# Reordering the operations of pairs 0 to 17 in a fused attention and feed-forward kernel

## The chip, the cores and the metric

The kernel runs on one core of a Trainium2 chip. The metric is device time in microseconds (us) of one execution; lower is better. Three executions of the kernel before were timed, and one was profiled.

## What is computed

The reference is a cosine attention over 8 batches, 12 heads, 448 positions and 64 elements a head, followed by a feed-forward block with a hard-swish:

```python
q_n = q / (np.linalg.norm(q, axis=-1, keepdims=True) + 1e-06)
k_n = k / (np.linalg.norm(k, axis=-1, keepdims=True) + 1e-06)
scores = np.matmul(q_n, k_n.transpose(0, 1, 3, 2)) / tau
attn = softmax(scores)                              # over the last axis
x = matmul(attn, v)  ->  (8 * 448, 12 * 64)          # heads side by side
h = x @ w_in                                        # 768 -> 2048
g = h * np.clip(h + 3.0, 0.0, 6.0) / 6.0
out = g @ w_out                                     # 2048 -> 768
```

Inputs and output are float32; the kernel multiplies in bfloat16.

## The kernel before

Heads are worked on two at a time: a batch has 6 pairs, the kernel 48 (pairs 0 to 47). Queries and keys come as items: item j holds the queries or the keys of two pairs, so items 2d and 2d+1 serve pairs 2d and 2d+1. The inverse norms of an item are taken along its elements, the item is scaled by them, transposed by TensorE (later ones by a transposing DMA), and copied out of PSUM as query and key tiles. A pair then has four groups of scores, four exponentials, four groups of values accumulated in one PSUM tile (PV), a division by the softmax sum, and a transpose back into xT, the input of the feed-forward block. When all six pairs of a batch are in xT, the first product of that batch can run (16 units, one per 128 columns of w_in, six matmuls each); each unit is evicted by ScalarE (relu, line 589) and then VectorE (product, line 595). When these are done, the second product follows.

Every operation of pairs 0 to 17 is written out by hand in a list of text lines, PLAN (lines 21 to 60). The function run takes its words in order, and do calls the function that the word names. Each engine has a queue in program order, so the order of the words is the order in every queue: TensorE, VectorE (v), ScalarE (a), GpSimd (p), and SyncE, which issues the loads of q, k, v and the transposing DMAs. Weight loads are issued by GpSimd. No scheduler moves anything; engines wait for each other by semaphores. From pair 18 on a loop issues the work (line 1012), and it is the same in both kernels.

The words that matter here, with numbers of items (j), pairs (i) or double items (d):

- LQ.j loads an item (line 197), LV.d the values of two pairs (line 212), W one piece of the weights (line 923).
- SQ.j.engine.first.n squares n columns of item j (lines 227 and 229); RE.j sums the squares on VectorE (line 241); NO.d takes the inverse norms of two items, with four steps on ScalarE (lines 269 to 276), or with a v at the end two steps on ScalarE and two on VectorE (lines 272 and 273). NO.0.0 and NO.0.1 are those of items 0 and 1 alone. NM.j.engine scales the item (line 286), with one more number for a half of it.
- TR.j transposes an item on TensorE (line 332) and XD.j by DMA; CQ.i and CK.i copy query and key tiles of a pair (lines 352 and 354), CS.i the rest of the keys. VC.i casts the values of a pair (line 305).
- SC.i.g are the four score groups of a pair (lines 432 and 435), EX.i.g their exponentials on ScalarE (line 453), VA.i.g the value groups (line 475), FI.i the division on VectorE (lines 495 and 496), BK.i and CX.i the transpose back and its copy into xT (line 509), XP and XB the same by DMA.
- U is the next feed-forward unit on TensorE (line 580 for the first product, line 627 for the second), UA and UV its next evictions on ScalarE and VectorE. The first 30 units are of the first product, the last six of the second.
- DP.n is n dummy matmuls on zeros (line 935), D.n the same with more columns (line 930). WS sums pieces of w_out and GL copies columns on VectorE for the later second product (lines 702 and 571).

Until the last exponential of pair 5 the scores use two double buffers of PSUM; from OPEN on they share a ring of six banks with the units, the transposes of items and the transposes back:

```python
m = [psum_m.tile([128, 512], FP32, name=f"M{n}", tag=f"M{n}") for n in range(4)]
ring.extend([m[0], m[1], Y, Z, m[2], m[3]])
```

A bank is taken again only when its readers of before are done. PV is one tile, so VA of a pair waits for FI of the pair before. The list of words that moves has only the function run and the table OPS between it and the engines.

Of the kernel before, what the change touches and what calls it, by code (L numbers as in the profile page):

```python
# [1110 lines left out]
```

## Time and profile before

| | |
|---|---|
| timed executions | 404.6, 406.22 and 406.69 us, median 406.22 |
| profiled execution, first to last instruction | 404.4 us (no time of its own beside this span is given) |
| TensorE busy | 393.7 us, 97% |
| VectorE busy | 288.7 us, 71% |
| ScalarE busy | 276.7 us, 68% |
| GpSimd busy | 236.7 us, 59% |
| bytes moved by DMA | 63.75 MB, mean 158 GB/s |

The timed executions include what lies around the span. Times inside the profile count from the first instruction. A row of a timeline gives the start, the time from the start of the first to the end of the last instruction of the row, the engine, the line, the operation, output and input, the number of instructions, and in brackets how long the engine sat idle before it and what ended that. Matmuls are pipelined and their ends are modelled, so the starts of successive rows, not their lengths, give the rate.

### The profile page before, as it was taken

The numbers are of one execution on the slowest core, as the hardware profiler recorded it, in microseconds if no ns is written. First come the engines' busy times: TensorE is split into PE (matmuls) and PEld (weight loads), VectorE is DVE, ScalarE is ACT, GpSimd is POOL, SyncE is SP. The second block draws the span as 40 slices with busy tenths as digits, with TensorE's granted clock in tenths as the row PEclk, the third lists the DMA queues.
The fourth block names the chain that finished last, engine by engine and source line by source line (L and its number), as shares of the span: only waits on it lengthen the run. The fifth ranks groups of instructions, "written<-read, shape, count | busy, mean of one in ns | idle before, by whom it ended". The sixth has DMA issues, their size and how long they took to land.

```text
span 404.4 us, 9618 instructions
## 1 busy us (share of the span) xinstructions
PE 393.7 (97%) x3689; PEld 234.5 (58%) x3689; DVE 288.7 (71%) x512; ACT 276.7 (68%) x604; POOL 236.7 (59%) x232
## 2 busy tenths in 40 slices
PE   7798999999999999999999999999999999999996
PEld 5566656555665555655555556555565556555564
DVE  5898787878498777777857887587656666655663
ACT  4899989887377687687768768768758755225230
POOL 4799945862744997588486875876664600510070
PEclk9999999999999999999999999999999999999999
DMA  8899999999877748786779659986863523140134
GB/s 285 247 235 243 221 221 213 170 219 202 181 168 179 167 111 209 185 222 129 169 200 194 140 149 163 180 190 136 193 147 76 112 45 63 36 88 20 25 74 99
DMA packets 93166, 63.75 MB, mean 158 GB/s; under 512 B 56128, under 2 KB 93120, under 8 KB 93120
## 3 DMA queue, kind: packets, MB, share of 16 engines
q1 hardware_dynamic: 87408, 56.45, 61.1%
q0 software_dynamic: 5312, 6.29, 9.5%
q8 instruction: 29, 0.48, 0.6%
q10 hardware_dynamic: 400, 0.39, 0.3%
q14 instruction: 17, 0.14, 0.1%
HBM read 45.61 MB, written 11.01 MB: 140 GB/s over the span
## 4 chain that ended last, share of the span: by engine, by line
PE 88%; ACT 4%; DVE 3%; DMA 3%; SPq 1%; issue 0%; DVEq 0%; ACTq 0%
PE M L580 23%; PE M L753 16%; PE PV L475 11%; PE Y L580 6%; PE Z L580 6%; PE M L435 6%; PE Z L753 5%; PE Y L753 4%; PE M L833 3%; PE M L627 3%; ACT at L453 3%; DMA big<-in_q_dram 3%; PE Y L435 1%; PE Z L435 1%; PE Y L833 1%; PE Y L627 1%
## 5 line engine op out<-in xcount | busy, mean ns | idle before, releaser
L453 ACT ACTIVATE at<-M 128x448 bf16<-128x448 f32 x194 | 96.8, 564 | 23.2 <-PE M L435 20.7
L580 PEld LDWEIGHTS <-w_in_sb 128*128 128x128 bf16 x768 | 72.3, 98 | 63.1 <-issue 2.5
L580 PE MATMUL M<-xT,w_in_sb 128*128 128x448 bf16 x504 | 107.4, 352 | 0.1
L286 POOL TENSOR_TENSOR nrm<-big,r 128x896 bf16<-128x896 f32 (+1 forms) x47 | 78.1, 1665 | 14.8 <-issue 4.6
L229 POOL TENSOR_TENSOR big<-big 128x896 f32<-128x896 f32 (+5 forms) x45 | 68.1, 1519 | 14.8 <-DMA big<-in_k_dram 8.2
L589 ACT ACTIVATE u<-M,bias 128x448 bf16<-128x448 f32 x84 | 54.9, 655 | 26.3 <-PE M L580 26.0
L475 PEld LDWEIGHTS <-at 128*128 128x128 bf16 (+1 forms) x1536 | 54.1, 97 | 19.9 <-issue 12.1
L595 DVE SCALAR_TENSOR_TENSOR gT<-u,M 128x448 bf16<-128x448 bf16 x73 | 44.6, 617 | 29.2 <-ACT u L589 28.4
L475 PE MATMUL PV<-vx,at 128*128 128x65 bf16 (+1 forms) x1536 | 62.7, 194 | 0.0
L241 DVE TENSOR_REDUCE n<-big 128x14 f32<-128x896 f32 (+1 forms) x50 | 51.5, 1037 | 0.3 <-ACT big L227 0.2
L392 POOL COPY km<-tT 64x128 bf16<-64x128 bf16 x34 | 14.4, 424 | 61.9 <-PE M L435 25.9
L782 POOL TENSOR_TENSOR big<-big 128x384 f32<-128x384 f32 x11 | 11.8, 1077 | 54.6 <-ACT big L801 54.5
L753 PEld LDWEIGHTS <-gT 128*128 128x128 bf16 x288 | 27.8, 98 | 20.0 <-DVE gT L731 0.6
L753 PE MATMUL M<-w_out_sb,gT 128*128 128x384 bf16 x192 | 35.0, 326 | 0.1
L496 DVE TENSOR_TENSOR on<-PV,rc 128x512 bf16<-128x512 f32 x48 | 33.2, 691 | 1.7
L435 PE MATMUL M<-tT,kz 64*128 64x448 bf16 (+1 forms) x171 | 30.9, 351 | 0.5 <-ACT at L453 0.5
L453 ACT ACTIVATE at<-Y 128x448 bf16<-128x448 f32 x50 | 28.2, 564 | 4.3 <-PE Z L435 4.3
L753 PEld LDWEIGHTS <-gs 128*128 128x128 bf16 x224 | 21.5, 98 | 14.7 <-DVE gs L731 0.3
L453 ACT ACTIVATE at<-Z 128x448 bf16<-128x448 f32 x50 | 28.2, 565 | 2.6 <-PE M L435 2.6
L305 POOL CAST vx<-big 128x512 bf16<-128x512 f32 x39 | 28.2, 728 | 3.1 <-DMA big<-in_v_dram 3.0
L580 PE MATMUL Z<-xT,w_in_sb 128*128 128x448 bf16 x132 | 28.6, 353 | 0.0
L580 PE MATMUL Y<-xT,w_in_sb 128*128 128x448 bf16 x132 | 28.6, 352 | 0.0
(128 smaller groups left out, 574.7 us busy)
## 6 DMA issues: line engine op xcount, KB each, us to landing
big<-in_k_dram SPq DMA_DIRECT2D x24, 448.0 KB, 5.1
big<-in_q_dram SPq DMA_DIRECT2D x24, 448.0 KB, 4.5
out_dram<-o SPq DMA_DIRECT2D x107, 96.0 KB, 2.2
big<-in_v_dram SPq DMA_DIRECT2D x48, 128.0 KB, 4.7
big<-in_v_dram SPq DMA_DIRECT2D x48, 96.0 KB, 4.4
w_in_sb<-in_moe_w_in_dram POOLq DMA_DIRECT2D x8, 384.0 KB, 10.4
w_out_sb<-in_moe_w_out_dram POOLq DMA_DIRECT2D x4, 768.0 KB, 10.8
tT<-nrm SPq DMA_TRANSPOSE x34, 2.8
```

What stands on the lines that cost most here:

```text
L229: engines[e].tensor_tensor(out=o, in0=i, in1=i, op=ALU.mult)
L241: nc.vector.tensor_reduce(out=n2_and_r[0][:, d % 2, j % 2, c], in_=sq[:, :, :, :].rearrange("p g c d -> p (g c) d")[:, c, :], axis=AX.X, o ...
L286: engines[e].tensor_tensor(out=nrm[:, :, g, :].rearrange("p c g d -> p g c d"), in0=raw_of[j][:, g, :, :], in1=n2_and_r[4][:, d % 2, j % 2, :]
L305: (engines[e].copy if e == "a" else engines[e].tensor_copy)(out=o, in_=f)
L435: nc.tensor.matmul(o, ks, qt[rows], start=True, stop=True)
L453: nc.scalar.activation(out=o, in_=x, func=AF.Exp, scale=inv_tau)
L475: nc.tensor.matmul(pv_out(j, h), at[rows, n, q_cols(i // HP, j)], vt[rows, 3 + h if name == "M" else 5 * h + int(name[1]), :], start=(name ...
L496: nc.vector.tensor_tensor(out=on[:, :, :, :].rearrange("p j h d -> p h j d"), in0=pv4[:, :, :, 0:D], in1=rc[:, :, :].to_broadcast([128, 2, ...
L580: nc.tensor.matmul(ps[:, 0:S], w_in_sb[:, cc, fc * 128 : (fc + 1) * 128], x[:, cc, 0:S], start=(cc == 0), stop=(cc == CC - 1),)
L589: nc.scalar.activation(out=u[:, :], in_=ps[:, 0:S], func=AF.Relu, bias=half_bias, scale=1.0 / 6.0)
L595: nc.vector.scalar_tensor_tensor(out=g[:, fc, c0 : c0 + S], in0=u[:, :], scalar=1.0, in1=ps[:, 0:S], op0=ALU.min, op1=ALU.mult,)
L753: nc.tensor.matmul(m, lhs[:, c, :], rhs[:, c, c0 : c0 + width], start=(base is None and c == 0), stop=(c == KC - 1), skip_group_check=True,)
```

## The change

Only PLAN changes. The words stand in another order, some operations go to another engine or are split otherwise, and there are 75 dummy matmuls in place of 87 and two wide ones. The work on real data is the same, operation for operation, with these moves among engines in the list: of the squares (in columns of an item, seven an item) GpSimd does more and ScalarE fewer; seven of the ten norms end on VectorE instead of two; VectorE scales six items instead of three and a half; ScalarE does 14 of the copies CQ, CK and CX instead of nine; GpSimd casts 15 of the 20 pairs' values instead of 11. The list is one line shorter, so every line number behind it is smaller by one in the kernel after.

In the old list the first scores (SC.0.0.0) stand behind the loads, squares or norms of items up to 4, and the first unit (U) behind all scores of pair 7. In the new list SC.0.0.0 stands behind items 0 and 1 and item 2's square, and the first U behind the scores of pair 6 and the transpose back of pair 5. The lines up to a little behind the first U, and the last ones:

```diff
@@ PLAN (lines 21 to 60 of the old text) @@
-    "DP.1 LQ.1 DP.2 DP.1 DP.1 DP.1 DP.1 DP.1 SQ.1.a.0.4 SQ.1.a.7.4 DP.1 SQ.1.v.4.3 DP.1 SQ.1.p.11.3 LQ.0 DP.2 DP.3",
-    "LQ.3 DP.1 LQ.2 SQ.0.p.6.2 RE.1.0 RE.1.1 LQ.5 DP.2 SQ.0.a.0.6 SQ.0.p.8.6 DP.1 RE.0.0 RE.0.1 DP.1 NO.0.1 DP.1 DP.1",
-    "NM.1.v.1 DP.1 SQ.3.a.0.7 DP.1 LQ.4 DP.2 D.2 DP.1 DP.2 NM.1.v.0 LV.0 DP.1 DP.2 NO.0.0.v DP.4 SQ.2.a.0.7 TR.1.Y",
-    "CK.1.a DP.1 DP.1 DP.1 DP.2 RE.3 DP.1 RE.2 NM.0.p.1 CK.0.a SQ.5.a.4.3 DP.2 DP.1 DP.4 DP.1 LQ.8 NM.0.p.0",
-    "SQ.4.v.4.3 SQ.5.a.0.4 NO.1 DP.1 DP.2 SQ.4.p.0.4 LV.1 TR.0.Z DP.3 DP.1 DP.1 NM.3.p LQ.7 NM.2.p.0 CQ.0.v SC.0.0.0",
-    "RE.5 LQ.6 DP.1 DP.1 EX.0.0 SC.0.1.1 DP.1 RE.4 NM.2.v.1 EX.0.1 DP.1 DP.1 NO.2 NM.4.p DP.1 LQ.10 VC.0.v DP.1 DP.2",
-    "LQ.9 DP.1 SC.0.2.0 SC.0.3.1 TR.3.Y CQ.1.v VC.1.v LV.2 CK.2.v DP.2 DP.2 DP.1 DP.1 VC.2.v EX.0.2 SQ.7.p.0.7 LQ.11",
-    "W EX.0.3 TR.2.Z CQ.2.v SC.1.0.0 EX.1.0 SC.1.1.1 CQ.3.v DP.1 SC.1.2.0 TR.4.Z VC.3.v EX.1.1 EX.1.2 SC.1.3.1 VA.0.0",
-    "CQ.4.v EX.1.3 DP.1 CQ.5.v LV.4 DP.2 LV.3 SQ.6.a.0.7 NM.5.v.1 W DP.1 DP.1 RE.7 SC.2.0.0 RE.6 VA.0.1 NM.5.p.0",
-    "SC.2.1.1 VA.0.2 VA.0.3 SQ.8.p.0.7 EX.2.0 EX.2.1 DP.3 SQ.9.p.0.7 DP.1 SC.2.2.0 FI.0 CK.3.v TR.5.Z SC.2.3.1 EX.2.2",
-    "CK.4.v NO.3.v NM.6.p RE.8 VA.1.0 VA.1.1 SC.3.0.0 VA.1.2 VA.1.3 EX.2.3 SC.3.1.1 FI.1 EX.3.0 SC.3.2.0 EX.3.1",
-    "EX.3.2 SC.3.3.1 EX.3.3 VA.2.0 SQ.10.p.0.7 RE.9 SQ.11.p.0.7 W NM.7.p.0 VC.4.p CK.5.v DP.1 VA.2.1 VA.2.2 VA.2.3",
-    "FI.2 VC.5.p LQ.13 NO.4 SC.4.0.0 TR.6.Y SC.4.1.1 EX.4.0 CQ.6.v CQ.7.v VA.3.0 VA.3.1 RE.10 VA.3.2 NM.8.p SC.4.2.0",
-    "BK.2.Z EX.4.1 EX.4.2 VC.6.p VA.3.3 NM.9.p W W VC.7.p LQ.12 LV.5 SC.4.3.1 SC.5.0.0 CX.2.v NM.7.v.1 FI.3 EX.4.3",
-    "BK.0.Y CX.0.v SC.5.1.1 EX.5.0 EX.5.1 SC.5.2.0 BK.3.Y DP.1 RE.11 TR.7.Z CX.3.v VA.4.0 VA.4.1 SQ.13.p.0.7 CK.6.v",
-    "SC.5.3.1 EX.5.2 BK.1.Y NO.5 NM.10.p EX.5.3 OPEN VA.4.2 CK.7.v SQ.12.p.0.7 SC.6.0 DP.1 CS.7.v VA.4.3 EX.6.0",
-    "CX.1.v CS.6.v SC.6.1 SC.6.2 TR.8 SC.6.3 EX.6.1 W W LQ.15 FI.4 VA.5.0 BK.4.Y VA.5.1 VA.5.2 CQ.8.v CQ.9.v EX.6.2",
-    "VC.8.p CX.4.v SC.7.0 VA.5.3 VC.9.p FI.5 TR.9 SC.7.1 EX.6.3 EX.7.0 SC.7.2 SC.7.3 CK.8.v CS.9.v CK.9.v VA.6.0",
-    "VA.6.1 CS.8.v VA.6.2 VA.6.3 BK.5 CX.5.v EX.7.1 SC.8.0 LQ.17 EX.7.2 EX.7.3 U EX.8.0 NM.11.p SC.8.1 SC.8.2 FI.6",
...
-    "SC.15.1 FI.14 LV.8 SC.15.2 WS.7.1 VC.15.a SC.15.3 U VA.15.0 EX.15.1 EX.15.2 CS.16.v EX.15.3 UA VA.15.1 VC.16.p",
-    "WS.1 SC.16.0 SC.16.1 VC.17.p SC.16.2 XD.19 EX.16.0 VA.15.2 VA.15.3 EX.16.1 LQ.23 U NM.18.p U VC.19.p XP.12",
-    "SC.16.3 CK.17.a LV.11 SQ.20.p.0.7 UA UV FI.15 WS.6 U XD.18 VA.16.0 VA.16.1 VC.18.p UV EX.16.2 EX.16.3 RE.20",
-    "SC.17.0 WS.y3 SC.17.1 SC.17.2 VA.16.2 XP.14 EX.17.0 EX.17.1 NO.10 SQ.22.v.0.4 EX.17.2 SQ.22.v.4.3 VA.16.3 LV.10",
-    "U FI.16 CK.18.v UA U WS.y4.0 SC.17.3 EX.17.3 CS.18.v CK.19.v UV XB.16 VA.17.0 NM.20.v",
+    "LQ.1 SQ.1.a.11.3 SQ.1.v.0.4 SQ.1.p.7.4 SQ.1.v.4.3 RE.1.0 LQ.0 SQ.0.a.6.2 SQ.0.a.8.6 RE.1.1 RE.0.1 SQ.0.p.0.6",
+    "RE.0.0 NO.0.1 NM.1.v.1 NM.1.p.0 LQ.3 DP.4 DP.4 DP.4 DP.4 DP.4 DP.4 DP.4 DP.4 DP.4 DP.2 TR.1.Y NO.0.0.v NM.0.p.0",
+    "NM.0.v.1 DP.4 TR.0.Z CQ.0.v CK.0.a LQ.2 SQ.2.p.0.7 DP.4 SC.0.0.0 SC.0.1.1 CK.1.v SQ.3.a.0.7 RE.3 LV.0 VC.0.p",
+    "EX.0.0 DP.4 DP.2 SC.0.2.0 EX.0.1 DP.3 SC.0.3.1 VA.0.0 W LQ.4 EX.0.2 CQ.1.v DP.1 SC.1.0.0 RE.2 SQ.4.p.4.3",
+    "SQ.4.v.0.4 VA.0.1 NO.1.v NM.3.v LV.1 VC.1.p NM.2.p.0 NM.2.v.1 EX.0.3 DP.2 SC.1.1.1 VA.0.2 VA.0.3 LQ.5 EX.1.0",
+    "SC.1.2.0 FI.0 VC.2.p SQ.5.p.0.4 DP.1 TR.3.Y CK.2.v EX.1.1 SC.1.3.1 EX.1.2 CK.3.a TR.2.Z RE.4 DP.1 VA.1.0 VC.3.p",
+    "SQ.5.p.4.3 BK.0.Y CQ.3.v LQ.6 SQ.6.p.0.7 CQ.2.a LQ.7 RE.5 SC.2.0.0 VA.1.1 EX.1.3 SQ.7.p.0.7 VA.1.2 LV.2 SC.2.1.1",
+    "EX.2.0 EX.2.1 VA.1.3 FI.1 SC.2.2.0 DP.3 SC.2.3.1 NO.2.v NM.5.p.0 NM.5.v.1 LQ.9 DP.2 VA.2.0 VA.2.1 EX.2.2 EX.2.3",
+    "SC.3.0.0 DP.1 SC.3.1.1 VA.2.2 EX.3.0 VA.2.3 CX.0.v EX.3.1 DP.2 TR.5.Z LV.4 CK.4.a LQ.10 SC.3.2.0 SC.3.3.1 RE.7",
+    "RE.6 LQ.8 LV.3 EX.3.2 BK.1.Y CK.5.v NM.4.p DP.2 TR.4.Z FI.2 CQ.4.v DP.2 VA.3.0 NO.3.v LQ.11 SC.4.0.0 EX.3.3",
+    "SC.4.1.1 W VA.3.1 VA.3.2 VA.3.3 CQ.5.a CX.1.v NM.6.v LQ.13 BK.2.Z EX.4.0 EX.4.1 SC.4.2.0 LQ.12 FI.3 TR.6.Y",
+    "SC.4.3.1 CX.2.v VC.4.p VA.4.0 CQ.7.v CQ.6.v VC.5.p VA.4.1 EX.4.2 EX.4.3 SC.5.0.0 SC.5.1.1 SQ.9.p.0.7 RE.9 VA.4.2",
+    "VA.4.3 BK.3.Y FI.4 NM.7.p.0 NM.7.p.1 LQ.14 EX.5.0 CX.3.v TR.7.Z CK.6.v SC.5.2.0 EX.5.1 DP.1 SC.5.3.1 CS.6.v",
+    "BK.4.Y EX.5.2 W SQ.8.p.0.7 VA.5.0 EX.5.3 OPEN SC.6.0 CS.7.v W VA.5.1 VA.5.2 VA.5.3 CK.7.a SQ.11.p.0.7 CX.4.v",
+    "VC.6.v EX.6.0 SC.6.1 EX.6.1 SC.6.2 SC.6.3 FI.5 DP.2 BK.5 CX.5.v U EX.6.2 VA.6.0 W W RE.8 SQ.10.p.0.7 EX.6.3 U UA",
+    "UV NO.4.v NM.8.p NM.9.p UA UV VA.6.1 SC.7.0 SC.7.1 U RE.10 EX.7.0 EX.7.1 SC.7.2 RE.11 UA SC.7.3 VA.6.2 UV EX.7.2",
...
+    "EX.14.3 U VA.14.0 VA.14.1 UA VC.17.a SC.15.0 EX.15.0 SC.15.1 SC.15.2 EX.15.1 LV.11 VA.14.2 VA.14.3 WS.6 U FI.14",
+    "SC.15.3 CK.17.v CS.16.v EX.15.2 XP.12 WS.1 VC.15.p LV.10 U NM.19.v EX.15.3 XD.19 UA VA.15.0 UV VA.15.1 CK.16.v",
+    "XD.18 SC.16.0 EX.16.0 RE.21 SC.16.1 SC.16.2 VA.15.2 EX.16.1 VC.18.v VA.15.3 U EX.16.2 SC.16.3 FI.15 UV VA.16.0",
+    "LQ.22 VA.16.1 WS.y3 EX.16.3 SC.17.0 EX.17.0 SC.17.1 SC.17.2 VA.16.2 RE.20 XP.14 EX.17.1 EX.17.2 VA.16.3 NO.10",
+    "FI.16 NM.20.p VC.19.p CK.18.v U U WS.7.0 WS.y4.0 UA UV SC.17.3 EX.17.3 CS.18.v CK.19.v SQ.22.p.4.3 WS.7.1",
+    "VA.17.0 SQ.22.a.0.4 GL.0 XB.16",
```

29 rows, old and new, of the table PLAN are left out of this document.

## The prediction

> **What bounds the kernel now.** I read the page first: its span, the engine totals and the chain that ended last.
>
> ```profile
> span 404.4 us, 9618 instructions
> PE 393.7 (97%) x3689; PEld 234.5 (58%) x3689; DVE 288.7 (71%) x512; ACT 276.7 (68%) x604; POOL 236.7 (59%) x232
> PE 88%; ACT 4%; DVE 3%; DMA 3%; SPq 1%; issue 0%; DVEq 0%; ACTq 0%
> ```
>
> TensorE is the bound by this reading, but its 97% counts dummy matmuls of the start (PV<-xT, line 935) as work. The question is how long TensorE runs before real work fills it, so I went on to the table of windows (TensorE, weight loads, VectorE, ScalarE, GpSimd, then granted clock, DMA share, GB/s), with borders that I took from the timelines below: first exponential, end of the first batch's exponentials, first feed-forward unit, about pair 12.
>
> ```profile
> 14.90:37.20 22.30, 20.16 (x284) 13.36 (x284) 21.43 (x46) 21.64 (x39) 21.73 (x19) 1.00 1.09 257
> 43.90:73.20 29.30, 29.20 (x321) 16.96 (x320) 22.83 (x49) 25.99 (x59) 19.64 (x18) 1.00 1.17 215
> ```
>
> From 14.90 to 37.20 ScalarE, VectorE and GpSimd are each busy 96 to 97%. From 43.90 to 73.20 TensorE is full. So the change, which touches only pairs 0 to 17, can win in two ways: real work earlier, and a lighter ScalarE until the first unit. It can lose by letting TensorE wait between 43.90 and 117.10. After pair 18 the code is the same, so what is won there shows at the end one for one. The timeline of TensorE gives the milestones:
>
> ```profile
> 2.47 5.55 PE L935 MATMUL PV<-xT 128*128 128x248 bf16 x26 [2.47 <-DVE vx L988]
> 8.40 1.22 PE L935 MATMUL PV<-xT 128*128 128x248 bf16 x10
> 9.46 0.55 PE L332 MATMUL Y<-ident,nrm 128*128 128x128 bf16 x7
> 12.36 0.56 PE L332 MATMUL Z<-ident,nrm 128*128 128x128 bf16 x7 [0.55 <-POOL nrm L286]
> 14.50 0.36 PE L435 MATMUL SC<-tT,kz 64*128 64x448 bf16 x2 [1.05 <-DVE tT L354]
> 43.90 1.31 PE L580 MATMUL M<-xT,w_in_sb 128*128 128x448 bf16 x6
> 55.09 0.36 PE L435 MATMUL M<-tT,kz 64*128 64x448 bf16 x2
> 55.39 0.56 PE L332 MATMUL Y<-ident,nrm 128*128 128x128 bf16 x7
> 55.79 0.35 PE L435 MATMUL Z<-tT,kz 128*128 128x448 bf16 x1
> 70.41 1.15 PE L475 MATMUL PV<-vx,at 128*128 128x65 bf16 x32
> 71.40 1.30 PE L580 MATMUL M<-xT,w_in_sb 128*128 128x448 bf16 x6
> 117.14 0.36 PE L435 MATMUL Y<-tT,kz 64*128 64x448 bf16 x1
> ```
>
> First scores at 14.50, first unit at 43.90, scores of pair 18 at 117.14. Prices, start to start: a score group up to 0.30 (55.09 to 55.39; taken as 0.25, since back to back it is less), a transpose of an item 0.40, a pair's values 0.99, so 0.25 a group.
>
> **Part 1, the first scores.** What held them in the old order:
>
> ```profile
> 5.49 0.52 ACT L227 ACTIVATE big<-big 128x384 f32<-128x384 f32 x1 [0.49 <-DMA big<-in_q_dram]
> 8.60 0.95 ACT L227 ACTIVATE big<-big 128x896 f32<-128x896 f32 x1 [1.63 <-DMA big<-in_k_dram]
> 10.66 0.95 ACT L352 COPY kz<-Y 128x448 bf16<-128x448 bf16 x2
> 10.47 1.83 POOL L286 TENSOR_TENSOR nrm<-big,r 128x448 bf16<-128x448 f32 x2 [3.75 <-DVE r L273]
> 7.29 1.15 DVE L286 TENSOR_TENSOR nrm<-big,r 128x448 bf16<-128x448 f32 x2
> 13.59 0.56 DVE L229 TENSOR_TENSOR big<-big 128x384 f32<-128x384 f32 x1 [1.27 <-DMA big<-in_q_dram]
> 14.06 0.38 DVE L354 COPY tT<-Z 128x448 bf16<-128x448 bf16 x1
> ```
>
> Item 0 landed at 5.49, but its norm on ScalarE stood behind the square of item 3, which began only at 8.60, when its load came. So GpSimd normalised item 0 only from 10.47 to 12.3. Its transpose was done at 12.9, and then VectorE sat in its queue on the square of item 4 (load there at 13.59) before the copy at 14.06. The new order puts items 2, 3 and 4 behind item 0's norm and behind that copy. Worked through with these durations: item 0 squared from 5.49, reduced by about 7.4; item 1's norm on ScalarE about 6.2 to 7.2; item 1 normalised on VectorE and GpSimd, half each, by 8.15; item 0's norm by 8.35; its halves (0.6 and 0.95) by 9.3. TensorE now has 38 dummies ahead of the first transpose: 26 at the slow 0.213 us end at 8.0 as before, the other 12 at the later rate (10 in 1.06, from 8.40 to 9.46) take 1.3. So the dummies, not the norm, start that transpose at 9.35. Four more dummies, item 0's transpose from 10.2 to 10.8, the copy, and the scores at 11.35, against 14.50. The square of item 3 fits on ScalarE before them, so the first exponential starts at about 11.8, not 14.90.
>
> [...]
>
> **Part 2, ScalarE until the first batch's exponentials end.** From the first one this engine sets the pace:
>
> ```profile
> 14.90 1.73 ACT L453 ACTIVATE at<-SC 128x896 bf16<-128x896 f32 x2 [0.99 <-PE SC L435]
> 21.84 0.97 ACT L227 ACTIVATE big<-big 128x896 f32<-128x896 f32 x1
> 22.68 2.66 ACT L453 ACTIVATE at<-SC 128x896 bf16<-128x896 f32 x3
> 25.24 0.22 ACT L269 ACTIVATE ln<-n 128x28 f32<-128x28 f32 x1
> 25.62 3.50 ACT L453 ACTIVATE at<-SC 128x448 bf16<-128x448 f32 x5
> 29.14 0.23 ACT L269 ACTIVATE ln<-n 128x28 f32<-128x28 f32 x1
> 30.20 5.50 ACT L453 ACTIVATE at<-SC 128x896 bf16<-128x896 f32 x7
> 36.65 0.53 ACT L453 ACTIVATE at<-SC 128x448 bf16<-128x448 f32 x1
> ```
>
> The stretch from 14.90 to 37.18 is 22.28 us. In it lie three four-step norms (29.14 to 30.20: 1.06 each), one norm that ends on VectorE (25.24 to 25.62: 0.38) and one square (21.84 to 22.68: 0.84), 4.40 together; the rest, 17.88, is six pairs, 2.98 each. The new order has the same six pairs, three of the short norms (1.14), no square, and four copies of 0.45 that were VectorE's (1.8): 20.8. To this I add 0.3 for item 4, which GpSimd normalises (a cast of values beside it):
>
> ```profile
> 34.03 1.16 POOL L305 CAST vx<-big 128x512 bf16<-128x512 f32 x2
> ```
>
> Its queue up to there holds squares and normalisings of 6.4 whole items at up to 1.83 (two halves above) and four casts at 0.58, some 14 us from 9.3, and 1 to 2 us of waits for loads; it ends at 24 to 25.5. Transpose and copy after it bring the scores to about 26.9, and pair 4 is due at 26.6. So the exponentials end at 11.8 + 20.8 + 0.3 = 32.9, against 37.18. Nothing of VectorE's share (three short norms' ends, 2.5 items more normalised there, fewer copies) is later than this in the same walk, but its margin is under 1 us.
>
> **Part 3, the first unit.** In the old order pair 7's scores, a group of pair 8, pair 6's values and the transposes of items 8 and 9 stand ahead of the first unit. In the new order only values, division, back transpose and copy of pair 5 do:
>
> ```profile
> 41.01 0.21 DVE L495 RECIPROCAL rc<-PV 128x8 f32<-128x8 f32 x1 [0.81 <-PE PV L475]
> 41.25 0.69 DVE L496 TENSOR_TENSOR on<-PV,rc 128x512 bf16<-128x512 f32 x1
> ```
>
> That is 0.4 for the last values, 0.9 for reciprocal and division, at most 0.4 for four transposes (seven take that) and 0.4 for a copy of the size of the one at 14.06, with about 0.9, an estimate, for what else stands in the two queues: 3.0. First unit at 35.9, 8.0 earlier. The work that it has overtaken is not saved: 5 score groups, 4 value groups and 2 item transposes are still to do, 5 x 0.25 + 4 x 0.25 + 2 x 0.40 = 3.05. Net 4.95.
>
> **Part 4, from there to pair 18.** If TensorE stayed as full as in the old order, pair 18 would start at 35.9 + (117.14 - 43.90) + 3.05 = 112.2. I do not believe all of it. Between the exponentials of pairs 6 and 12 the new order gives ScalarE 6 x 2.98 for pairs, 14 evictions, five copies, three short norms, a long one and a cast. An eviction takes at most 0.59:
>
> ```profile
> 95.26 1.18 ACT L589 ACTIVATE u<-M,bias 128x448 bf16<-128x448 f32 x2
> ```
>
> That is 17.9 + 8.3 and 5 for the rest, some 31 us in about 34; in the old order's stretch of 29.30 only four pairs lie beside 14 evictions. With six PSUM banks TensorE runs at most about 3 us ahead of ScalarE, so two nearly full engines wait for each other at times. I take 1.2 us (0 to 3). The second loss lies behind pair 15's first exponential. There VectorE sums weights, and TensorE runs units of the second product:
>
> ```profile
> 111.39 1.75 DVE L702 TENSOR_TENSOR w_out_sb<-w_out_sb 128x3072 bf16<-128x3072 bf16 x1
> 111.41 5.36 PE L627 MATMUL M<-w_out_sb,gT 128*128 128x384 bf16 x32
> ```
>
> The new order has three whole and three half sums there (5.3 and, at two thirds each, 3.5), three divisions (2.7) and some 7 us of reductions, copies and evictions: 18.5. TensorE has 22 groups at 0.25 and five units of 2.6 (5.36 for two, less the last one's tail): 18.5 as well, where the old order had seven units, six of them this long. The division of each pair queues behind these sums, and the next pair's values wait for it. I take 1.15 (0 to 2.5). Edits with one answer: moved loads and weight DMAs stand on SyncE's and GpSimd's queues at nothing, hidden by the items already loaded; if that cover goes, rival D is the price.
>
> **Sum.** 4.95 - 1.2 - 1.15 = 2.6. The profiled span goes from 404.4 to 401.8. The runs' median 406.22 lies 1.8 above that span, and I keep this distance: 403.6. About 0.5% (2 us, the spread of the three runs) is what a measurement of this kernel can tell from no change.
>
> **The rivals.** A is the forecast, 402.4 to 405: 0.40.
> B: nothing is lost after the first unit, 406.2 - 4.95 = 401.2. For it: TensorE stood at 29.20 of 29.30 even with ScalarE at 25.99. Against: the tighter ScalarE. 0.14.
> C: the losses eat the gain, 406 (ends of both ranges, 3 + 2.5 of 4.95): 0.18.
> D ends slower: item norms are now late, and the units are spent while TensorE waits for them. Place: items 8 and 9, which GpSimd normalises by about 42.3 in my walk and TensorE wants at about 43.9, a margin of 1.6; all later items stand in the same queue.
>
> ```profile
> 62.56 1.68 POOL L229 TENSOR_TENSOR big<-big 128x896 f32<-128x896 f32 x1 [6.97 <-DMA big<-in_k_dram]
> ```
>
> In the old order GpSimd once waited 6.97 for an item's load without harm. The same wait ahead of item 8 or 9 would pass 6.97 - 1.6 = 5.4 on to TensorE: 403.6 + 5.4 = 409.0. It decides once GpSimd is later than 43.9, and beats the gain from 4.2 on. 0.25.
> E: TensorE falls back to half clock in the start. [...] 0.03.
>
> **Range and chances.** 8 in 10 takes A, B, C and most of D: 399.8 to 409.5; alone, A spans 402.4 to 405. Faster by over 0.5%: three quarters of A, all of B, a little of C: 0.50. Within 0.5%: 0.21. Slower: most of D, E and a little of C: 0.29.
>
> **What would show it.** In the changed profile: first scores near 11.3, first exponential near 11.8, end of pair 5's exponentials near 33, first unit (line 579) near 36, scores of pair 18 near 114.5, then 287 us as before. A wrong Part 1 shows as TensorE waiting for a normalised item rather than for dummies; a wrong Part 4 as TensorE idle behind ScalarE's evictions or VectorE's division (B: none; C: over 4 us); D as TensorE's transposes waiting for GpSimd between 40 and 65.

## The result, and the profile after

The changed kernel takes 417.04 us (415.41 to 418.33, four executions) beside 406.1 for the kernel before on the same chip: a ratio of 1.0288, 95% interval 1.0246 to 1.0331. Forecast were 403.6, at most 409.5. Here and below a median counts every execution, and a ratio leaves out those that took over 1.5% longer than the fastest of the same kernel. The profiled execution took 417.98 us and has this span, engine totals and last chain (lines are smaller by one than before):

```profile
span 415.8 us, 9594 instructions
PE 395.6 (95%) x3675; PEld 234.2 (56%) x3675; DVE 294.6 (71%) x516; ACT 275.6 (66%) x598; POOL 241.0 (58%) x234
PE 79%; DVE 8%; DMA 5%; ACT 4%; POOL 1%; issue 1%; SPq 0%; POOLq 0%; DVEq 0%; ACTq 0%
```

Work on each engine is nearly what it was. What changed is the chain: TensorE's share falls from 88% to 79%, VectorE and DMA together gain 7 points. The milestones in TensorE's timeline, to be laid beside those of before:

```profile
2.48 6.86 PE L934 MATMUL PV<-xT 128*128 128x248 bf16 x38 [2.48 <-DVE vx L987]
9.18 0.55 PE L331 MATMUL Y<-ident,nrm 128*128 128x128 bf16 x7
11.89 0.56 PE L434 MATMUL SC<-tT,kz 64*128 64x448 bf16 x4
42.49 1.30 PE L579 MATMUL Y<-xT,w_in_sb 128*128 128x448 bf16 x6
125.88 0.36 PE L434 MATMUL Y<-tT,kz 64*128 64x448 bf16 x1
```

First scores at 11.89 (forecast 11.35, before 14.50), first unit at 42.49 (forecast 35.9, before 43.90), pair 18 at 125.88 (forecast 114.5, before 117.14). So the early lead is real and is gone long before the first unit. The windows (TensorE, weight loads, VectorE, ScalarE, GpSimd, clock, DMA share, GB/s) for the two stretches of the prediction:

```profile
12.29:40.00 27.71, 22.50 (x305) 14.71 (x303) 22.22 (x46) 21.14 (x34) 25.32 (x24) 0.94 1.02 248
42.49:73.20 30.71, 29.77 (x324) 17.02 (x321) 26.58 (x55) 27.32 (x65) 26.22 (x21) 1.00 0.93 209
```

In the first, ScalarE was 97% busy before and is now 76% busy; only GpSimd (91%) is nearly full. In the second, GpSimd has 26.22 us where it had 19.64: its work on items has slid behind the first unit.

To place the loss I added up TensorE's useful matmuls (dummies left out, each shape at one price, 367 us in all) in both traces, and took the difference of the times at which the same sum was done. After minus before: -3.7 us in pair 1, +1.4 at the first units, +4.1 ahead of pair 13, +9.2 behind it, 8.6 ahead of the loop, +11.5 from its entry to the end. The three stretches follow.

**Pairs 1 to 5.** ScalarE's timeline:

```profile
12.29 2.54 ACT L452 ACTIVATE at<-SC 128x896 bf16<-128x896 f32 x3 [1.09 <-PE SC L434]
20.70 0.53 ACT L351 COPY kz<-Y 128x448 bf16<-128x448 bf16 x1 [2.65 <-DVE kz L353]
21.94 0.53 ACT L351 COPY tT<-Z 128x448 bf16<-128x448 bf16 x1 [0.70 <-DVE tT L353]
28.38 1.73 ACT L452 ACTIVATE at<-SC 128x896 bf16<-128x896 f32 x2 [1.35 <-PE SC L434]
36.72 3.05 ACT L452 ACTIVATE at<-SC 128x896 bf16<-128x896 f32 x4 [0.27 <-PE SC L434]
```

Its first exponential is where it was forecast, and pair 5's last one ends at 39.8 instead of 32.9. ScalarE's own work between is the forecast 20.8; the rest, 6.3 us, is waiting, 3.8 of it (2.65, 0.70 and 0.49) in front of copies that share a PSUM bank with copies of VectorE and stand behind them. TensorE and VectorE at the first of these:

```profile
19.53 0.27 PE L934 MATMUL PV<-xT 128*128 128x248 bf16 x1 [2.53 <-DVE on L495]
19.63 0.55 PE L331 MATMUL Y<-ident,nrm 128*128 128x128 bf16 x7
25.16 0.78 PE L934 MATMUL PV<-xT 128*128 128x248 bf16 x3 [0.73 <-DVE on L495]
```

```profile
16.26 2.37 DVE L285 TENSOR_TENSOR nrm<-big,r 128x896 bf16<-128x896 f32 x2
18.55 0.20 DVE L494 RECIPROCAL rc<-PV 128x8 f32<-128x8 f32 x1
18.78 0.69 DVE L495 TENSOR_TENSOR on<-PV,rc 128x512 bf16<-128x512 f32 x1
20.22 0.39 DVE L353 COPY kz<-Y 128x448 bf16<-128x448 bf16 x1 [0.75 <-PE Y L331]
```

The transpose of item 3 stands in TensorE's queue behind a dummy. The dummies write PV, so behind pair 0's last values a dummy waits for pair 0's division, and that stands on VectorE behind 2.37 us of normalising items 3 and 2. And TensorE's granted clock was 0.51 from 25.00 to 28.41:

```profile
21.59:25.00 3.41, 1.98 (x32) 1.31 (x31) 2.10 (x5) 3.03 (x6) 3.32 (x2) 1.00 1.11 235
25.00:28.41 3.41, 3.25 (x26) 1.80 (x25) 3.31 (x7) 1.49 (x4) 2.58 (x2) 0.51 1.07 272
```

**Pair 13.** GpSimd issues four pieces of w_out, 3 MB, between 71.8 and 76.4 (three together, one behind them), in the same 5 us in which SyncE issues the transposing DMAs of items 15 and 14:

```profile
71.83 2.31 POOL L922 DMA_DIRECT2D w_out_sb<-in_moe_w_out_dram  x3
75.55 0.81 POOL L922 DMA_DIRECT2D w_out_sb<-in_moe_w_out_dram  x1
71.91 5.58 SPq L342 DMA_TRANSPOSE tT<-nrm  x2
```

The DMA view from 68 to 95 gives, as median us from issue to landing, first after:

```profile
w_out_sb<-in_moe_w_out_dram POOLq DMA_DIRECT2D x4, 768.0 KB, 18.8
tT<-nrm SPq DMA_TRANSPOSE x2, 14.8
```

and before:

```profile
w_out_sb<-in_moe_w_out_dram POOLq DMA_DIRECT2D x2, 768.0 KB, 10.0
tT<-nrm SPq DMA_TRANSPOSE x4, 3.4
```

Two of the four transposes before are those of items 15 and 14; each landed 2.65 us after its issue at 76.0 and 77.3. After the change they took 11.3 and 18.2 us. Who waits for that, in the timelines of VectorE and TensorE after:

```profile
91.46 0.35 DVE L381 COPY kz<-tT 128x384 bf16<-128x384 bf16 x1 [3.41 <-DMA tT<-nrm]
91.73 0.61 DVE L594 SCALAR_TENSOR_TENSOR gT<-u,Z 128x448 bf16<-128x448 bf16 x1
92.40 1.54 PE L579 MATMUL Z<-xT,w_in_sb 128*128 128x448 bf16 x6 [3.18 <-DVE gT L594]
93.73 2.45 PE L579 MATMUL M<-xT,w_in_sb 128*128 128x448 bf16 x6
```

VectorE's queue is blocked by a key copy whose transpose has not landed; the product behind it frees no bank; TensorE stands still for 3.18 us, and the unit after that takes 2.45 instead of 1.30, since the granted clock is 0.50 from 93.3 to 96.7. With the rows around it that is the 5.1 us of the lag.

**The loop's entry.** VectorE sums weights there, and ScalarE's half of item 22's square waits for its load:

```profile
127.32 0.63 ACT L226 ACTIVATE big<-big 128x512 f32<-128x512 f32 x1 [1.04 <-DMA big<-in_k_dram]
127.56 0.36 PE L434 MATMUL M<-tT,kz 64*128 64x448 bf16 x2 [1.14 <-DVE o L639]
129.19 1.90 DVE L570 COPY gT<-gT 128x1024 bf16<-128x1024 bf16 x1
134.03 1.64 PE L752 MATMUL M<-w_out_sb,gT 128*128 128x384 bf16 x9 [1.58 <-DVE gT L594]
```

### The profile page after: what moved, and what is told of

The parts are those of the page before. It is cut to its first block, busy times and chain, and to the rows that moved or that the text cites. A ratio compares the mean times of both kernels' runs of the same rounds, so it can differ in the third digit from the quotient of the medians.

```text
span 415.8 us, 9594 instructions
## 1 busy us (share of the span) xinstructions
PE 395.6 (95%) x3675; PEld 234.2 (56%) x3675; DVE 294.6 (71%) x516; ACT 275.6 (66%) x598; POOL 241.0 (58%) x234
## 4 chain that ended last, share of the span: by engine, by line
PE 79%; DVE 8%; DMA 5%; ACT 4%; POOL 1%; issue 1%; SPq 0%; POOLq 0%; DVEq 0%; ACTq 0%
PE M L579 18%; PE M L752 15%; PE PV L474 10%; PE Z L579 6%; PE Y L579 5%; PE Z L752 5%; DMA tT<-nrm 4%; PE M L434 4%; PE Y L752 3%; PE M L832 3%; PE M L626 3%; ACT at L452 2%; DVE on L495 1%; DVE n L240 1%; DVE nrm L285 1%
## 5 line engine op out<-in xcount | busy, mean ns | idle before, releaser
L452 ACT ACTIVATE at<-M 128x448 bf16<-128x448 f32 x198 | 99.0, 565 | 24.0 <-PE M L434 23.2
L579 PE MATMUL M<-xT,w_in_sb 128*128 128x448 bf16 x474 | 102.3, 356 | 0.0
L285 POOL TENSOR_TENSOR nrm<-big,r 128x896 bf16<-128x896 f32 (+1 forms) x45 | 75.4, 1679 | 25.0 <-ACT r L275 18.1
L228 POOL TENSOR_TENSOR big<-big 128x896 f32<-128x896 f32 (+4 forms) x45 | 71.4, 1588 | 15.7 <-DVE n L240 9.7
L588 ACT ACTIVATE u<-M,bias 128x448 bf16<-128x448 f32 x79 | 51.7, 657 | 29.9 <-PE M L579 25.7
L594 DVE SCALAR_TENSOR_TENSOR gT<-u,M 128x448 bf16<-128x448 bf16 x68 | 41.6, 618 | 31.0 <-ACT u L588 30.3
L579 PE MATMUL Y<-xT,w_in_sb 128*128 128x448 bf16 x162 | 35.1, 353 | 0.0
L434 PE MATMUL M<-tT,kz 64*128 64x448 bf16 (+1 forms) x174 | 32.0, 354 | 1.9 <-DVE o L639 1.1
L304 POOL CAST vx<-big 128x512 bf16<-128x512 f32 x43 | 32.0, 745 | 2.3 <-DMA big<-in_v_dram 2.2
L579 PE MATMUL Z<-xT,w_in_sb 128*128 128x448 bf16 x132 | 28.8, 355 | 3.2 <-DVE gT L594 3.2
L452 ACT ACTIVATE at<-Y 128x448 bf16<-128x448 f32 x46 | 26.0, 566 | 4.3 <-PE Z L434 4.3
```

The lines of the kernel that those rows point to most:

```text
L228: engines[e].tensor_tensor(out=o, in0=i, in1=i, op=ALU.mult)
L285: engines[e].tensor_tensor(out=nrm[:, :, g, :].rearrange("p c g d -> p g c d"), in0=raw_of[j][:, g, :, :], in1=n2_and_r[4][:, d % 2, j % 2, :]
L304: (engines[e].copy if e == "a" else engines[e].tensor_copy)(out=o, in_=f)
L434: nc.tensor.matmul(o, ks, qt[rows], start=True, stop=True)
L452: nc.scalar.activation(out=o, in_=x, func=AF.Exp, scale=inv_tau)
L579: nc.tensor.matmul(ps[:, 0:S], w_in_sb[:, cc, fc * 128 : (fc + 1) * 128], x[:, cc, 0:S], start=(cc == 0), stop=(cc == CC - 1),)
```

## The experiments

The kernel before took 404.3 to 404.4 us (medians) beside them; ratios and their 95% intervals are to that. Each is an edit of the list of words of the kernel after, unless another is named.

**No dummies behind pair 0's first values.**

```diff
-DP.n   (all 12 words behind VA.0.0, 20 dummies)
```

> The changed kernel without the 27 dummy matmuls that stand behind the first values (VA.0.0). They write into PV, so from there on a dummy waits for the division of the pair before, and all of TensorE's queue waits behind it (2.53 us at 17.0 and 0.73 at 24.4 in the changed kernel). Theory (three separate waits that the order places): the transposes of items 2 and 3 start at about 18 instead of 19.63, the first unit comes 2 to 3 us earlier than 42.5, and the run is 2 to 3 us faster than the changed kernel (about 414.5). Rival (the order is simply too tight, ScalarE and VectorE nearly full, the waits only show it): the wait moves to the next instruction, first unit within 0.7 us of 42.5 and the time within 1 us of 417. Third possibility: without dummies TensorE's clock falls to half in this stretch and the run is slower, 418 to 420.

Measured: 415.0, ratio 1.0184 (1.0121 to 1.0247). The edit took out 20 dummies, not the 27 of the expectation. The waits for the division went and the first unit came at 41.3, but TensorE ran at half clock from 20.2 to 27.0 (a score group of two matmuls took 0.55 us there, 0.36 outside). The dummies' wait exists. That the clock falls for longer without them is not shown: runs below that keep them have 0, 3.4 or 6.8 us of half clock in the start.

**The weight burst taken apart.**

```diff
-EX.12.1 EX.12.2 W W W CX.10.v ... EX.13.2 W SQ.19.v.4.3
+NM.12.p W W ... EX.12.1 EX.12.2 CX.10.v ... EX.13.2 SQ.19.v.4.3 ... SQ.19.p.0.4 W W
```

> The changed kernel with the four w_out loads (768 KB each) apart: two behind the normalising of item 12, two behind the second half of item 19's square, instead of three in a row and a fourth just ahead of the transposing DMAs of items 15 and 14. Theory: those two transposes, which landed after up to 18 us, land in under 8; VectorE's key copy of pair 15 no longer waits 3.41 us, TensorE's 3.18 us at 89.2 and the slow matmuls behind it (1.54 and 2.45 us for six, else 1.30) go; the run is 4 to 5 us faster than the changed kernel (about 412.5). Rival: the transposes are late because their items are late (normalised at 71.9), not because of the weights; then they land hardly earlier, and the time stays within 1 us of 417.

Measured: 411.07, 1.0152 (1.0122 to 1.0183), the largest single gain. The wait at pair 13 is gone; the lag stays at 3.3 us there, with nothing of the 5. But the transposes did not land in under 8 us, as the theory had it. The DMA view from 68 to 95:

```profile
tT<-nrm SPq DMA_TRANSPOSE x2, 13.2
```

The first landed at 83.8, where it had landed at 83.3; the second came at 86.2 instead of 91.4, and that was early enough for VectorE's copy.

**The late sums earlier.**

```diff
-U U WS.7.0 WS.y4.0 ... SQ.22.p.4.3 WS.7.1 VA.17.0 SQ.22.a.0.4 GL.0
+WS.6 GL.0 WS.7.0 ... FI.15 WS.7.1 ... U U WS.y4.0 ... SQ.22.p.4.3 VA.17.0 SQ.22.a.0.4
```

> The changed kernel with GL.0 and the two half sums of weight 7 moved ahead on VectorE, GL.0 and the first half behind WS.6, the second half behind FI.15, where VectorE is idle for 1.95 and 1.73 us. Theory: the waits of TensorE at 126.4 (1.14, for VectorE's eviction) and 132.5 (1.58, for the product of a unit) go, and the run is 2 to 2.7 us faster than the changed kernel (about 414.5), with pair 18 starting at about 125.9 as before. Rival (VectorE is full from pair 15 on): the sums now delay the division of pairs 14 and 15 instead, pair 18 starts later by what the loop gains, and the time stays within 1 us of 417.

Measured: 414.04, 1.0221 (1.0187 to 1.0255). The waits for VectorE at the entry went, and 1.15 for ScalarE came in their place: its square of item 22, behind a late load. In this profile the burst, still in place, cost far less than in that of the kernel after, 1.6 us of lag and no half clock; its second transpose landed at 89.2:

```profile
90.19 1.29 PE L579 MATMUL Z<-xT,w_in_sb 128*128 128x448 bf16 x6 [1.20 <-DVE gT L594]
```

**All three edits, and the second with the third.**

> The three edits together. Theory: they add up, 8 to 10 us less than the changed kernel, so 407 to 409, level with the kernel before or up to 3 us above it; what is left is the loss between pairs 6 and 12. Rival: the waits replace each other and the sum is under 5 us: 412 or more.

> The changed kernel with the weights apart and the sums earlier, and with its dummies. Alone they gave 5.0 and 2.0 us (1.0152 and 1.0221 of the kernel before, where the change has 1.0288); with the dummies out all three together gave only 1.0193, and half-clock windows stood in that profile. Theory (the waits are separate, and taking the dummies out is what spoiled the sum, by the clock): the two add up, 1.0288 - 0.0136 - 0.0067, so about 1.0085, 408 us where the kernel before has 404.4. Rival (the waits replace each other): no better than the weights alone, 1.015.

Measured: 412.87, 1.0193 (1.0147 to 1.0239), and 411.73, 1.0169 (1.0137 to 1.0201). Neither is better than the weights alone. Both have 6.8 us of half clock in the start, which the weights alone had not; the first has 3.4 more at 123.7 (mean granted clock 0.988 and 0.989, and 0.998 with the weights alone). The edits do not add up, and the wait for item 22 remains at the entry (1.84 and 1.25 us in these profiles). Half clock comes and goes from execution to execution (the four of the first kernel have mean granted clocks from 0.986 to 0.996); a stretch of 3.4 us at a granted 0.51 would cost a full TensorE 1.7 us (an estimate from these two numbers), but in the start it cost less. Five profiled executions have this same start: the first unit is at 41.55 without half clock, at 41.97, 42.26 and 42.49 with one such stretch, at 42.92 with two. And the execution of the second kernel with two of them took 411.61, the three others, at a mean clock of 0.995 or 0.996 for 0.989, 411.47 to 412.23, so half clock is not what kept the two gains from adding up.

**Dummies moved, not removed**, on top of the last:

```diff
-DP.1 TR.3.Y ... DP.1 VA.1.0 ... SC.2.2.0 DP.3 SC.2.3.1 ... DP.2 VA.2.0 ... DP.1 SC.5.3.1 ... VA.5.0
+TR.3.Y ... VA.1.0 DP.2 ... SC.2.2.0 SC.2.3.1 ... VA.2.0 DP.5 ... SC.5.3.1 ... VA.5.0 DP.1
```

> As e5_weights_and_sums, and the dummies that wait for a division ahead of other work (before TR.3.Y, SC.2.3.1, SC.5.3.1 and VA.1.0) stand behind the next values instead, as many as before. Theory: the transposes of items 3 and 2 start at about 17.4 as they did without dummies, but the first unit gains only about 0.7 us, since the copies on ScalarE still wait for VectorE's copy out of the same bank, which stands behind the division; the clock stays up, so 0.5 to 1 us faster than e5. Rival (the dummies are the whole loss of the first stretch): the first unit comes 2 us or more earlier than in e5.

Measured: 410.82, 1.0147 (1.0112 to 1.0181); item 3's transpose at 17.47 instead of 19.63, first unit at 41.03, full clock in the start. With only the weights apart, also at full clock, the first unit was at 41.55. So the dummies' wait is worth about 0.5 us there, and the half clock of the kernel after the other 0.9 of its 42.49.

**Copies of one bank on one engine**, on top of that:

```diff
-CK.2.v ... CQ.3.v ... CK.5.v ... CQ.4.v
+CK.2.a ... CQ.3.a ... CK.5.a ... CQ.4.a
```

> As e6_dummies_behind, and the copies of query and key tiles of pairs 2 to 5, of which the new order gives one of each two to ScalarE and one to VectorE, are all on ScalarE (four more of 0.45 us). Theory (two engines that read one bank are kept in turn, so ScalarE waits for VectorE's late queue: 2.65, 0.70 and 0.49 us before these copies in the changed kernel): ScalarE's waits at 18 to 22 and 32 us go, the exponentials of pair 2 start at about 20.5 instead of 22.9, the first unit comes at 39 to 40 instead of 41.5 to 42.5, and the time falls another 1.5 to 2.5 us, to about 405 to 406. Rival (ScalarE is the bound and four more copies cost their 1.8 us): first unit within 0.7 us of e6, no gain or 1 us slower.

Measured: 410.05, 1.013 (1.0098 to 1.0162); first unit at 41.27 with 3.4 us of half clock in the start, and 40.99 with the same start at full clock (in the run below with item 22's load earlier): no earlier than 41.03. The copies did not hold the first unit. At the entry this wait was left, which had been 1.50 us with the dummies moved alone:

```profile
122.61 1.29 PE L579 MATMUL Y<-xT,w_in_sb 128*128 128x448 bf16 x6 [0.93 <-ACT at L452]
```

**The kernel before with the burst.**

```diff
 SQ.16.p.6.1
+W W W W   (its last four weight loads, moved here)
```

> The kernel before with its four w_out loads in one row on GpSimd (at about 68 us, behind item 16's square) instead of two at 64 and two at 80. Theory: the transposing DMAs of items 14 and 15, which land in about 5 us in the kernel before, now land behind 3 MB of weights, after 10 to 15 us; VectorE's key copies at 81.6 come 3 to 6 us later and the kernel is 2 to 5 us slower than before. Rival (the weights do not matter; in the changed kernel these items were simply late): within 0.5% of the kernel before.

Measured: 415.04, 1.0274 (1.022 to 1.0329). The same place in TensorE's timeline:

```profile
91.54 2.40 PE L580 MATMUL Z<-xT,w_in_sb 128*128 128x448 bf16 x6 [6.95 <-DVE gT L595]
```

and 6.8 us of half clock. The transposes took 13.3 and 14.9 us. Four moved words in the old order cost 10.6 us, twice the most that the theory expected and as much as the whole change. What a burst costs is thus no fixed price: 1.6 us of lag in the profile of the sums earlier, 5.1 in the kernel after, 9.9 here.

**The new order to the first unit, then the old, and the reverse.**

```diff
 ... FI.5 DP.2 BK.5 CX.5.v          (the new list up to here)
-U EX.6.2 VA.6.0 W W RE.8 SQ.10.p.0.7 EX.6.3 U UA UV NO.4.v ...
+RE.8 SQ.10.p.0.7 NO.4 RE.10 NM.8.p NM.9.p W VC.7.p ...   (what is left, in the old order)
```

> The new order up to the first unit, then all that is left in the old order (one exponential, that of pair 6's last group, one place earlier, because its bank is wanted). Theory S (each stretch carries its own loss): at the first unit the changed kernel is 1.4 us behind the old one at equal work, and the rest is the old order, so 404.4 + 1.4 = 405.8; 404 to 407.5, the upper end with one stretch of half clock of 3.4 us. Rival T (the start leaves arrears on ScalarE and GpSimd that come due between pairs 6 and 11): the 3 us that are lost there come too, 408.8 or more.

The reverse, on the kernel before:

```diff
 ... LQ.17 EX.7.2 EX.7.3            (the old list up to here)
-U EX.8.0 NM.11.p SC.8.1 SC.8.2 FI.6 ...
+LQ.14 U U UA UV UA UV U U UA UV U W FI.6 ...   (what is left, in the new order)
```

> The mirror image: the old order up to the first unit, then all that is left in the new order (one exponential of pair 8 a few places earlier). Theory S: the losses behind the first unit stay, 3.0 between pairs 6 and 11, 5 at pair 13, 2.7 at the loop's entry less the old kernel's own: 416 less 1.4 = 414.6; 413 to 416. Rival T: without the arrears of the new start only the burst at pair 13 and the entry stay, 411 to 412.

Measured: 417.94, 1.0328 (1.0297 to 1.036), and 410.54, 1.011 (1.0074 to 1.0147). Both answer for arrears, the rival; the first has far more of them than it expected. With the new start and the old rest, TensorE has nothing to do in front of item 8, and 10.2 us of half clock behind it (TensorE, then GpSimd):

```profile
48.09 0.93 PE L331 MATMUL Y<-ident,nrm 128*128 128x128 bf16 x7 [4.95 <-POOL nrm L285]
```

```profile
46.35 3.33 POOL L285 TENSOR_TENSOR nrm<-big,r 128x896 bf16<-128x896 f32 x2
```

Items 8 and 9 are normalised there from 46.35 on. The kernel after has them no earlier; the kernel before had them from 35.16 and 37.36:

```profile
46.38 3.34 POOL L285 TENSOR_TENSOR nrm<-big,r 128x896 bf16<-128x896 f32 x2 [0.48 <-DVE r L272]
```

```profile
35.16 1.68 POOL L286 TENSOR_TENSOR nrm<-big,r 128x896 bf16<-128x896 f32 x1
37.36 1.68 POOL L286 TENSOR_TENSOR nrm<-big,r 128x896 bf16<-128x896 f32 x1
```

So the new start leaves the items' norms some 11 us late, and the early units of the new rest cover that. In the profile of the old start with the new rest the loss between pairs 6 and 11 is 1.5 us, where the kernel after lost about 3. (That profiled execution took 415.95 us, the longest of five, with the burst's wait of 4.40 us and 3.4 us of half clock at pair 13; the others lay between 408.2 and 410.7.)

**The load of item 22 earlier**, on top of the copies together:

```diff
+LQ.22 LQ.23 ...
-FI.15 UV VA.16.0 LQ.22 VA.16.1
+FI.15 UV VA.16.0 VA.16.1
```

> The kernel with copies together (410.05), and the load of item 22 issued ahead of that of item 23, some 90 operations earlier. Theory: ScalarE's square of item 22 was what pair 18's score waited for in the last three kernels (0.93 to 1.50 idle on TensorE); it goes, 409.0, 408.5 to 409.5. Rival: VectorE's late weight sums, beside GpSimd's half of the same square, become the last to arrive, and the time stays at 410 within 0.5; then the idle at the entry is put down to VectorE.

Measured: 408.72, 1.0103 (1.0083 to 1.0122): within the theory's 408.5 to 409.5. No wait on TensorE of more than 0.2 us is left between pair 15 and pair 18.

**The new order to pair 12, then the old.**

```diff
 ... EX.11.3 LQ.21 VA.11.0 VC.12.p   (the new list up to here)
-EX.12.0 SC.12.1 SC.12.2 VA.11.1 UA UV NM.15.p XD.15 ...
+(what is left, in the old order)
```

> The new order up to pair 12's first exponential, then what is left in the old order (with two operations earlier, for their banks): the four late weight loads and the entry of the loop are as before, the start and pairs 6 to 11 as in the changed kernel. Theory S: the lag at that place, 4.5 us, is all that is left: 408.9; 407.5 to 410.5. Rival T: arrears of the start and the middle still come due at the loop's entry, 2.7 more, 411.6.

Measured: 413.79, 1.0224 (1.0194 to 1.0255), above both theories, by 4.9 and 2.2. The profiled execution had 6.2 us of lag from pair 12 on, 2.2 of them a wait of TensorE at the seam itself (79.39, for VectorE's product) that neither order has, and 3.4 us of half clock in the start. Behind the seam it lost hardly anything more. It says little on the middle by itself.

**Which part of the start, and what is left with the old one.**

```diff
 ... SQ.3.a.0.7 RE.3 LV.0 VC.0.p EX.0.0   (the new list up to here)
-DP.4 DP.2 SC.0.2.0 EX.0.1 DP.3 SC.0.3.1 VA.0.0 ...
+LQ.5 LQ.4 RE.2 SQ.5.a.4.3 LQ.8 SQ.4.v.4.3 SQ.5.a.0.4 NO.1 ...   (what is left, in the old order)
```

> The new order up to pair 0's first exponential, then everything that is left in the old order, old dummies included. Theory P (the early first scores are sound and the order behind them makes the norms late): first exponential at 12.3, no wait for an item's norm behind it, first unit no later than in the old kernel, at 42 to 43, and the time 402 to 405 against 404.3 before. Rival Q (the first two items' norms, put ahead, push those of items 2 to 5 back by themselves): pair 2's exponentials start no earlier than 22, TensorE waits for GpSimd's or VectorE's normalising before the first unit, and the time is 407 or more.

The old list to the first unit and then the new, with the three edits from above (weights apart, sums earlier, LQ.22 earlier), and the kernel before unchanged:

> The old order up to the first unit, then the new order (410.54 by itself) with the late weight loads in two places, the late sums earlier and item 22's load earlier. Theory P: the 4.4 us wait at pair 13 with its half clock and the waits of 1.6 and 1.1 at the loop's entry go; what is left is 1.5 us between pairs 6 and 11: 404.3 + 1.5 = 405.8, 405 to 407. Rival Q: the new order behind the first unit pays only with the new start's early units; waits of ScalarE's evictions come in, 408 to 410.

> The kernel before, unchanged. If the late loads in the profile that the forecast was made from belong to that one execution, the first exponential is at about 12.7, as in the kernel with the weight burst, and the span near 402.3; if they belong to the kernel, at 14.9, and the span is 404.4.

Measured for the first: 409.56, 1.0132 (1.0087 to 1.0177), the rival's outcome. ScalarE, then TensorE:

```profile
12.32 0.92 ACT L452 ACTIVATE at<-SC 128x896 bf16<-128x896 f32 x1 [1.17 <-PE SC L434]
20.77 2.97 ACT L452 ACTIVATE at<-SC 128x896 bf16<-128x896 f32 x4 [1.58 <-PE SC L434]
```

```profile
16.13 0.38 PE L431 MATMUL SC<-tT,kz 64*64 64x448 bf16 x2 [2.41 <-ACT at L452]
17.34 0.91 PE L331 MATMUL Y<-ident,nrm 128*128 128x128 bf16 x7 [0.83 <-POOL nrm L285]
```

The first exponential is at 12.32, but pair 1's come at 20.77, later than the 19.01 of the profile before: items 2 to 5 must still be squared, reduced and normalised. Pair 0's fourth scores wait for its second exponential, which stands behind squares of item 5 and the norms of items 2 and 3 on ScalarE, and the transpose behind them waits for GpSimd's normalising. The first unit is at 45.59. Half clock from 17.4 to 20.8 accounts for part of this, by the estimate above for at most 1.7 us, which is about all that this execution lags behind (1.7 us at equal work). So the splice shows that the lead of 2.6 us in the first exponential is lost by pair 1; that more than the lead is lost, it does not show.

For the second: 406.74, 1.0053 (1.003 to 1.0076), as the theory had it. For the third: 406.17 against 404.35 for the same kernel beside it, 1.0028 (1.0009 to 1.0048), which is how finely two kernels can be told apart here. Mended, with the old start, the new order's rest is hardly distinguishable from the old. The kernel before is the fastest of all that ran.

The third, with the other runs of the old start, also shows what the base of the forecast was worth, though not as either theory had it. ScalarE in it, and in the old order with the burst (whose start is the same):

```profile
9.07 0.95 ACT L227 ACTIVATE big<-big 128x896 f32<-128x896 f32 x1 [2.15 <-DMA big<-in_k_dram]
15.64 1.73 ACT L453 ACTIVATE at<-SC 128x896 bf16<-128x896 f32 x2 [0.74 <-PE SC L435]
```

```profile
6.84 0.93 ACT L227 ACTIVATE big<-big 128x896 f32<-128x896 f32 x1
12.68 1.73 ACT L453 ACTIVATE at<-SC 128x896 bf16<-128x896 f32 x2
```

The loads of items 3 and 4 land when they land. Five profiled executions have the old start: VectorE squares its part of item 4 from 10.72, 12.98, 12.99, 13.59 and 14.33 on, in all but the first when the load arrives, and the first exponential follows at 12.68, 14.29, 14.30, 14.90 and 15.64, in these four 1.31 us later each time. The first unit is then at 42.17, 43.90, 43.96, 43.90 and 45.24. So 14.90 was no rare draw; 12.68 is the exception. The new start, whole or in part, has its first exponential between 12.23 and 12.40 in all of its 12 profiled executions.

## Why the prediction was wrong, point by point

**Part 1, the first scores: right.** 38 dummies gate the first transpose (9.18, forecast 9.35), scores at 11.89 (11.35), first exponential at 12.29 (11.8). The gain was taken against one execution, and it holds against four of five (14.29 to 15.64); in the fifth, where the loads of items 3 and 4 came early, the old start's first exponential was at 12.68, and the lead only 0.4.

**Part 2, ScalarE: its work right, its wait wrong.** 20.8 us of work was measured as forecast; the term "0.3 for item 4" was 6.3. The step that failed is the sentence that nothing of VectorE's share is later than the walk. The walk priced each engine's work and let the items' norms keep up, while the new order had put the squares of items 3 to 5 behind the first scores. Item 4, which it let GpSimd finish by 24 to 25.5, was normalised by 28.8; even so its transpose, at 31.68, waited last for a copy of VectorE and not for it, and pair 4's scores, due at 26.9, began at 33.07. Two single waits (dummies behind the division, copies behind VectorE's) were in the rows, but taking them away brought the first unit 0.5 us and nothing; half clock explains another 0.9. For the rest the rows point to VectorE's and GpSimd's time for norms: GpSimd is 91% busy in this stretch, and in the splice behind the first exponential the lead is gone by pair 1, with TensorE waiting behind norms. This is argued and not shown: no run gave these norms more time, and which of the two engines' queues sets the pace in pairs 2 to 5 was not separated.

GpSimd's walk was short for a second reason. Where VectorE normalises at the same time, GpSimd's halves took 1.31 to 1.86 us (five in the kernel after and one in the kernel before, all before 36 us), against 0.94 to 0.95 where it does not (one and four):

```profile
16.35 1.80 POOL L285 TENSOR_TENSOR nrm<-big,r 128x448 bf16<-128x448 f32 x1
```

```profile
23.18 0.95 POOL L286 TENSOR_TENSOR nrm<-big,r 128x448 bf16<-128x448 f32 x1
```

The rows are of the kernel after and of the kernel before. So each such half took 0.4 to 0.9 us longer, and the new order, which normalises 2.5 items more on VectorE, has five of them where the old has one. Why GpSimd takes longer there is not shown.

**Part 3, the first unit: wrong by 6.6 us** (42.49 for 35.9), wholly inherited from part 2. From the end of pair 5's exponentials to the first unit it took 2.7 us, for a forecast of 3.0. The overtaken work of 3.05 us stood to be done, so a net gain of 4.95 became a lag of 1.4. That is the largest part of the miss.

**Part 4.** The term for pairs 6 to 12, 1.2 (0 to 3), measured about 3 by pair 11 and 2.7 ahead of pair 13. With the old start 1.5 was left of it, so half was arrears of the start. The forecast's mechanism, TensorE waiting for ScalarE, is in the other half (that six banks let TensorE run about 3 us ahead was my estimate, which no run measured); this wait stands, at 0.92 or 0.93 us, in all 12 profiled executions that have the new order there:

```profile
73.92 0.35 PE L434 MATMUL Y<-tT,kz 64*128 64x448 bf16 x1 [0.92 <-ACT at L452]
```

The term behind pair 15, 1.15 (0 to 2.5), measured 2.9; the mechanism (VectorE's sums) was there, but the late load of item 22, which I had put at nothing, stood behind it with nearly the same price. The second large failure is the sentence "edits with one answer: moved loads and weight DMAs ... at nothing". Four weight loads moved in front of two transposing DMAs cost 5.1 us by the trace and 5.5 by the runs (ratios 1.0288 and 1.0152). Named as its price was rival D, which is GpSimd's lateness; what came due was the time of transposing DMAs beside queued loads, which the prediction had no row for and did not bound.

Together, from the forecast 2.6 us ahead to the 11.5 behind at equal work: 6.35 in the start, 1.5 in pairs 6 to 12, 5.1 at pair 13, 1.75 at the loop's entry, less 0.6 won back between the last two.

**The rivals.** D's mechanism was there, and wider than it was put: items 8 and 9 were normalised by 49.7 instead of 42.3, well beyond its point of 43.9. In the kernel after, the units in front hid it: TensorE began those transposes, at 48.12 and 49.77, without idling. The old rest, without these units, paid 4.95 at once, half clock behind it, and a time of 417.94. E, half clock in the start, had 0.03; that it was so unlikely, no trace of before shows. It came in the start of 9 of the 12 profiled executions whose start is the new one, whole or in part. One stretch of it lasted 3.41 us at a granted 0.51 (the kernel after), and moved the first unit by 0.4 to 0.9 us.

In runs, the way back: the burst apart 411.07; with the sums, dummies and copies 410.05; item 22's load 408.72; the old start 406.74; the old kernel 404.35.

## What to carry to other kernels

An early milestone is worth nothing until the next thing in the same stretch is also early: price the supply (here the norms of the items behind) for several steps beyond the one that is moved, not the consumer alone. When transfers move in an order written by hand, list what is issued within the next 20 us on every other queue, transposing DMAs above all (2.65 us each in the kernel before, 11.3 and 18.2 in the kernel after), and give it a price with a range instead of nothing. And look at a second execution before taking a gain from a wait for a load.
